# A retention and gated-MLP kernel: own output buffers and earlier transposes for the last batches, norms of first halves moved, last output unit in halves, another order in the head

## The chip, the cores and the metric

The kernel runs on one core of a Trainium2 chip. The metric is the device time of one execution in microseconds (us). Three runs of the kernel before gave 229.06, 230.06 and 230.72 us; their median, 230.06 us, is the time that the change is measured against. A difference of about 1% is what a measurement can tell from no change.

The engines are named as in the profile: PE (matrix multiply) with its weight loads PEld, DVE (vector), ACT (scalar), POOL (GpSimd) and SP, which here only issues transfers. Every engine works through its own list of instructions in order; semaphores connect the lists.

## The reference

Eight batches of eight heads, 576 positions, head width 64. Retention is attention without a softmax: the scores are weighted with a causal decay that has its own rate for each head. A gated MLP follows, whose gate mixes positions with a 576 x 576 matrix.

```python
scores = scale * np.matmul(q, k.transpose(0, 1, 3, 2))          # (8, 8, 576, 576)
Dmat = np.where(rel >= 0, gamma[:, None, None] ** rel, 0.0)      # rel = i - j
x = np.matmul(scores * Dmat, v)                                  # -> (8, 576, 512)
h = gelu_tanh(x @ w_in)                                          # (8, 576, 1024)
u, v = h[..., :512], h[..., 512:]
v_n = (v - mean(v)) / np.sqrt(var(v) + 1e-6) * g_ln
v_s = np.einsum('ts,bsd->btd', w_sg, v_n) + b_sg[None, :, None]
out = x + (u * v_s) @ w_out
```

## The kernel before

**Tiling.** The decay is split into one factor on q and one on k, so that retention becomes a running state. The 8 x 576 positions are worked off in 18 blocks. A group of four batches has one lead block (the first 64 positions of all four) and then two blocks of 256 positions for each batch, a first half and a second half. A block holds two chunks of 128 positions, c = 0 and 1. Two batches form a pair p with nine chunks; chunk 4 (`MID`) holds the leads of both. Blocks 10 to 17 are batches 4 to 7; the last two belong to batch 7.

**Steps of a block j.** `load` fetches q, k and v into the pool `ld` (three buffers of each tag; q and k share one tile of tag "qk", v has tag "vf"). `cast` scales them to bf16, on POOL from block 3 on. `T` (PE) or `turn` (a transposing transfer on SP's queue) transposes q and k. `Sc` makes the scores on PE and masks them on DVE (`ret`, L320). `Z` adds to the state and copies it to bf16 (`zb`, L344). `inter` and `intra` give the retention output in PSUM; two copies on ACT bring it to `xT` (L377). These copies go through the helper `copy`, so that the profile shows them under L245. `V` (L381) makes the second half of h: four matmuls `hv`, the gelu on ACT (`vg`), then `stats` on DVE (`bst`, `mv`, `rs`, and `vc`, which is the centred value times g_ln), `power` on POOL (`rs` to the power -1/2, L392) and `norm` on ACT (`vn`, or `vnm` for the lead chunk). `U` makes the first half (`hu`, `uT`).

**Steps of a batch.** When its second block is through, `release` queues eight units `W` (L440: the mixing of positions, five matmuls each, then a DVE product `gT`) and its units `O` (L459: four matmuls with w_out, the residual x, and the output transfer). `run(n)` takes n units from that queue at fixed places of a block; `slots` holds these numbers. A `W` needs the `vn` of all five chunks of its batch.

**The residual in O.** Where no transposed x is there, four matmuls with the identity add x in PSUM (L469) and ACT copies to `ob`. For batches 5 to 7 `turn_x` (L292) has asked SP's queue for the transpose of `xT`, and DVE adds it (L473). `ob` has three buffers for all units (pool `w3`); an `ob` is free again when its output transfer has ended.

**What sets the order.** The program is written out by hand, step by step (from L504; the blocks 3 to 17 in the loop at L627). `later(n, f)` (L231) postpones f by n ticks; each `T`, `V`, `U`, `W` and `O` ends with a tick. In the loop `stats` comes 2 and `norm` 4 ticks after `V`. In the head (blocks 0 to 2) they are called by name from `stats_of`, `pow_of` and `norm_of`. PSUM buffers of tag "d" (three) are shared by `hv`, `hu`, `wp` and `op`.

**The head** also prepares constants: `split_b` splits the bias into three bf16 rows, `place_b(e)` writes them into `wL[e]` with three small transfers issued by POOL, `load_w` fetches w_sg, `build_wT` transposes it, and `w_in` is cast by ACT and POOL. `spin(n)` issues n matmuls of zeros whose result nobody reads.

Of the kernel before, what the change touches and what calls it, by code (L numbers as in the profile page):

```python
# [19 lines left out]
def kernel(  # L20
# [77 lines left out]

    srow_i = consts.tile([128, 3, 2], I32, name="srow_i")
    nc.gpsimd.iota(srow_i[:, 0], pattern=[[1, 2]], base=0, channel_multiplier=2)  # L100
    nc.gpsimd.iota(srow_i[:, 1:], pattern=[[256, 2], [1, 2]], base=LEAD, channel_multiplier=2)
# [64 lines left out]
    bp = consts.tile([SB * 2, 3, 64], BF, name="bp")  # L166

# [122 lines left out]
    xns = {}  # L290
# [34 lines left out]
    def Z(j, c):  # L325

        gr, b, half = place(j)
        if b is None or (half, c) == (1, 1):
            nb = GB * gr if b is None else b + 1
            if c == 0 or nb == GB * (gr + 1):  # L330
                return
            src, lo, n, first = blk[NPG * gr], 32 * (nb % GB), 32, True
            zcur[0] = psZ.tile([128, KK, D], F32, name="zp")
        else:
            src, lo, n, first = blk[j], 64 * c, 64, False
        z, rows = zcur[0], slice(lo, lo + n)
        for a in range(2):
            for kk in range(KK):
                for r in range(2):
                    h = 2 * kk + r  # L340
                    nc.tensor.matmul(z[64 * r:64 * r + 64, kk, :], src["kb"][rows, a, h, :], src["vb"][rows, a, h, :],  # L341
                                     start=(first and a == 0 and kk == 0), stop=True, skip_group_check=True)
# [36 lines left out]
    stats_of, pow_of, norm_of = {}, {}, {}  # L379

    def V(j, c, wait=(2, 4)):  # L381
# [12 lines left out]
        def stats():  # L394
# [6 lines left out]
            st["rs"] = rs  # L401
            if wait:
                power()
            vc = w2.tile([128, F2], F32, name="vc")
# [15 lines left out]
        if wait:  # L420
            later(wait[0], stats)
            later(wait[1], norm)
        else:
            stats_of[2 * j + c], pow_of[2 * j + c], norm_of[2 * j + c] = stats, power, norm
# [34 lines left out]
    def O(p, m):  # L459
        op = psD.tile([128, DM], F32, name="op", tag="d")  # L460
        r = slice(128 * m, 128 * m + 128)
        xn = xns.get((p, m))
        for c in range(KK):
            nc.tensor.matmul(op[:], gTs[p][:, c, r], w_out[:, c, :], start=(c == 0),  # L464
                             stop=(xn is not None and c == KK - 1), skip_group_check=True)
        ob = w3.tile([128, DM], F32, name="ob")
        if xn is None:
            for kk in range(KK):
                nc.tensor.matmul(op[:, 128 * kk:128 * kk + 128], xTs[p][:, m, kk], ident[:],  # L469
                                 start=False, stop=True, skip_group_check=True)  # L470
            nc.scalar.copy(ob[:], op[:])  # L471
        else:
            nc.vector.tensor_tensor(ob[:], op[:], xn, op=Alu.add)  # L473
        if m == MID:
            for e in range(2):
                nc.sync.dma_start(out[2 * p + e, :LEAD, :], ob[64 * e:64 * e + 64])
        else:
            s0 = LEAD + 128 * (m % (MID + 1))
            nc.sync.dma_start(out[2 * p + (m > MID), s0:s0 + 128, :], ob[:])
# [34 lines left out]
    split_b()  # L514
# [10 lines left out]
    nc.gpsimd.memset(wnat[:, :, 0:64], 0.0)  # L525
    place_b(0)
# [5 lines left out]
    T(1, "q")  # L532
    cast(1, "v", nc.gpsimd)
# [3 lines left out]
    cast(2, "k", nc.gpsimd)  # L537
    inter(1)
# [3 lines left out]
    cast(2, "q", nc.vector)  # L542
    T(2, "k")
# [6 lines left out]
    for n in range(2):  # L550
        (nc.gpsimd.tensor_copy if n else nc.scalar.copy)(w_in[:, :, 256 * n:256 * n + 256], w_stage[0][:, :, 256 * n:256 * n + 256])
# [3 lines left out]
    Z(2, 0)  # L555
    inter(2)
    fill_first()
    stats_of[0]()
    pow_of[0]()
    Sc(2, 1)  # L560
    Z(2, 1)
    cast(3, "k", nc.gpsimd)
# [5 lines left out]
    U(0, 1)  # L568
    intra(2)
    U(1, 0)  # L570
    norm_of[2]()
    stats_of[3]()
    cast(3, "q", nc.gpsimd)
    pow_of[3]()
    V(2, 0, None)
    V(2, 1, None)
    load(5)
    build_wT(wb[0])
    norm_of[3]()
    U(1, 1)  # L580
    build_wT(wb[1])
    stats_of[4]()
    cast(3, "v", nc.gpsimd)
    place_b(1)
    pow_of[4]()
    build_wT(wb[2])
    U(2, 0)
    build_wT(wb[3])
    stats_of[5]()
    pow_of[5]()  # L590
    norm_of[4]()
# [28 lines left out]
    later(14, stats_of[1])  # L620
    later(16, pow_of[1])
# [5 lines left out]
    for j in range(HEAD, NB):  # L627
        nx = j + 1 < NB
        slots = where[share.get(j, 6)]
# [15 lines left out]
        if not nx:  # L645
            V(j, 1)
        run(slots[1])
# [15 lines left out]
        for x in {NB - 4: (NB - 6, NB - 5), NB - 3: (NB - 4,), NB - 2: (NB - 3, NB - 2), NB - 1: (NB - 1,)}.get(j, ()):  # L663
            turn_x(x)
# [37 lines left out]
```

## Time and profile before

| what | value |
|---|---|
| median of three runs (lowest, highest) | 230.06 us (229.06, 230.72) |
| the profiled execution's own time | 228.41 us |
| its span in the profile | 226.6 us |
| busy PE / DVE / POOL / ACT | 205.2 / 165.7 / 129.4 / 125.3 us |
| moved by transfers | 47.34 MB, mean 209 GB/s |
| longest groups by busy time on PE | `wp` 41.7, `hu` 37.8, `hv` 35.1, `op` 34.8 us |

A row of the timeline gives the start (us from the span's start), the busy time, the engine, the line, the operation with its output and inputs, and the count; in square brackets stands how long the engine was idle before it, and what ended that. A row of the windows gives a stretch, its length, and each engine's busy time in it with the number of instructions; then the clock granted to PE (1.00 is full), the share of time that the transfer engines were busy, and GB/s. A row of the waits gives the total idle time in us, the number of waits and the longest. The profiled execution took 1.8 us more than its span, and 1.65 us less than the median of the three runs.

### The profile page before, as it was taken

What the parts mean: (1) busy time and instruction counts of PE and PEld (TensorE: products, weight loads), DVE (VectorE), ACT (ScalarE), POOL (GpSimd) and SP (SyncE); (2) the same over time, 40 slices, a digit from 0 to 9 for tenths busy, and PEclk for the clock granted to TensorE, in tenths of its full rate; (3) what the DMA queues carried; (4) which work ended last, traced back from release to release, by engine and by line L of the source; (5) the groups of instructions that cost most, each with busy time, mean ns of one, the idle gap of its engine ahead of it and who ended that gap; (6) DMA issues with size and microseconds to landing.
All of it is one profiled execution on the core that took longest, in us unless ns stands there. A gap on an engine that the chain in (4) does not pass through costs nothing.

```text
span 226.6 us, 8008 instructions
## 1 busy us (share of the span) xinstructions
PE 205.2 (91%) x3391; PEld 145.5 (64%) x3427; DVE 165.7 (73%) x356; ACT 125.3 (55%) x202; POOL 129.4 (57%) x130
## 2 busy tenths in 40 slices
PE   7796998789999799999999799999999999799990
PEld 2444575577677587677677676777767766566650
DVE  5456599778969797469857866769856987777852
ACT  5353467715576755856594848675565546265110
POOL 5298759799956595729483847648482811113000
PEclk9999699999999999999999999999999999999998
DMA  7999999999999699799959999999989934822334
GB/s 174 279 304 277 304 254 280 278 248 227 168 243 298 166 201 208 235 204 314 220 168 275 235 208 146 241 245 258 222 228 200 133 69 117 210 49 46 139 99 183
DMA packets 87492, 47.34 MB, mean 209 GB/s; under 512 B 25440, under 2 KB 81824, under 8 KB 87456
## 3 DMA queue, kind: packets, MB, share of 16 engines
q1 hardware_dynamic: 84896, 45.10, 87.4%
q0 software_dynamic: 1472, 1.20, 3.4%
q10 hardware_dynamic: 1088, 0.52, 1.0%
q8 instruction: 27, 0.44, 0.9%
q14 instruction: 9, 0.07, 0.1%
HBM read 32.79 MB, written 9.44 MB: 186 GB/s over the span
## 4 chain that ended last, share of the span: by engine, by line
PE 54%; DMA 17%; POOL 11%; DVE 6%; ACT 4%; issue 3%; ACTq 1%; DVEq 0%; SPq 0%; POOLq 0%
PE wp L454 14%; PE op L464 9%; PE hv L385 9%; PE hu L434 9%; DMA qk<-in_q_dram 6%; DMA qk<-in_k_dram 5%; DMA out_dram<-ob 4%; POOL rs L392 3%; PE sc L316 3%; POOL kb L263 2%; PE ot L368 2%; PE ot L357 2%; PE zp L341 2%; POOL qb L263 2%; PE tp L272 2%
## 5 line engine op out<-in xcount | busy, mean ns | idle before, releaser
L392 POOL TENSOR_TENSOR rs<-rs,mhalf 128x1 f32<-128x1 f32 x36 | 33.0, 918 | 68.8 <-DVE rs L400 68.7
L320 DVE TENSOR_TENSOR ret<-sc,mask 128x512 bf16<-128x512 f32 x72 | 46.1, 683 | 9.6 <-PE sc L316 9.6
L454 PE MATMUL wp<-wT,vn 128*128 128x288 bf16 x256 | 41.7, 286 | 2.9 <-DMA wL<-bp 1.3
L434 PE MATMUL hu<-xT,w_in 128*128 128x128 bf16 x576 | 37.8, 219 | 1.4 <-DVE ob L473 1.4
L385 PE MATMUL hv<-w_in,xT 128*128 128x512 bf16 x125 | 35.1, 380 | 3.9 <-ACT xT L245 2.9
L434 PEld LDWEIGHTS <-w_in 128*128 128x128 bf16 x576 | 34.1, 98 | 4.1 <-issue 1.5
L456 DVE TENSOR_TENSOR gT<-wp,uT 128x288 bf16<-128x288 f32 x64 | 28.1, 452 | 11.6 <-PE wp L454 10.2
L396 DVE BATCH_NORM_STATS2 bst<-vg 128x6 f32<-128x512 f32 x36 | 24.8, 689 | 15.9 <-ACT vg L388 15.7
L464 PE MATMUL op<-w_out,gT 128*128 128x512 bf16 x129 | 34.8, 380 | 1.1 <-issue 0.5
L417 ACT ACTIVATE vn<-vc,rs 128x512 bf16<-128x512 f32 x32 | 23.1, 722 | 19.5 <-POOL rs L392 18.3
L263 POOL TENSOR_TENSOR kb<-qk,gk 128x1024 bf16<-128x1024 f32 x16 | 30.9, 1930 | 2.5 <-DMA qk<-in_k_dram 2.4
L405 DVE SCALAR_TENSOR_TENSOR vc<-vg,mv,g_bc 128x512 f32<-128x512 f32 x36 | 31.5, 875 | 0.2 <-issue 0.2
L454 PEld LDWEIGHTS <-vn 128*128 128x128 bf16 x256 | 23.8, 98 | 11.2 <-ACT vn L417 3.6
L388 ACT ACTIVATE vg<-hv 128x512 f32<-128x512 f32 x36 | 21.3, 595 | 16.8 <-PE hv L385 16.6
L263 POOL TENSOR_TENSOR qb<-qk,gq 128x1024 bf16<-128x1024 f32 x15 | 29.0, 1931 | 0.0
L437 ACT ACTIVATE uT<-hu 128x512 bf16<-128x512 f32 x36 | 21.7, 602 | 12.3 <-PE hu L434 12.2
L471 ACT COPY ob<-op 128x512 f32<-128x512 f32 x24 | 14.0, 589 | 19.8 <-PE op L469 19.0
L245 ACT CAST xT<-ot 128x512 bf16<-128x512 f32 x33 | 22.0, 730 | 2.1 <-PE ot L368 2.1
L385 PEld LDWEIGHTS <-xT 128*128 128x128 bf16 x144 | 13.0, 98 | 15.7 <-ACT xT L245 5.1
L245 ACT COPY kT<-tp 128x1024 bf16<-128x1024 bf16 x15 | 15.1, 1007 | 8.8 <-PE tp L272 8.8
L464 PEld LDWEIGHTS <-gT 128*128 128x128 bf16 x144 | 12.5, 98 | 10.9
L454 PE MATMUL wp<-wL,vnm 128*128 128x288 bf16 x64 | 18.4, 287 | 0.0
(96 smaller groups left out, 264.8 us busy)
## 6 DMA issues: line engine op xcount, KB each, us to landing
qk<-in_k_dram SPq DMA_DIRECT2D x16, 512.0 KB, 6.2
qk<-in_q_dram SPq DMA_DIRECT2D x16, 512.0 KB, 7.8
vf<-in_v_dram SPq DMA_DIRECT2D x16, 512.0 KB, 7.1
out_dram<-ob SPq DMA_DIRECT2D x32, 256.0 KB, 3.3
wst<-in_moe_w_in_dram SPq DMA_DIRECT2D x2, 1024.0 KB, 7.8
vf<-in_v_dram SPq DMA_DIRECT2D x8, 128.0 KB, 4.5
out_dram<-ob SPq DMA_DIRECT2D x8, 128.0 KB, 2.4
qk<-in_k_dram SPq DMA_DIRECT2D x6, 128.0 KB, 3.4
```

What stands on the lines that cost most here:

```text
L245: (eng.copy if eng is nc.scalar else eng.tensor_copy)(o, i)
L263: eng.tensor_tensor(o, src, tab[:, kind].rearrange("p a h -> p h a").unsqueeze(3).to_broadcast([128, H, 2, D]), op=Alu.mult)
L320: nc.vector.tensor_tensor(s["ret"][:, r, 2 * g:2 * g + 2], sc[r][:], msk[:].unsqueeze(1).to_broadcast([128, 2, 2, 128]), op=Alu.mult)
L385: nc.tensor.matmul(hv[:], xTs[p][:, m, kk], w_in[:, kk, F2:], start=(kk == 0), stop=(kk == KK - 1))
L392: nc.gpsimd.tensor_tensor(st["rs"][:], st["rs"][:], mhalf[:], op=Alu.pow)
L396: nc.vector.bn_stats(bst[:], vg[:])
L405: nc.vector.scalar_tensor_tensor(vc[:], vg[:], mv[:, 0:1], g_bc[:], op0=Alu.subtract, op1=Alu.mult)
L417: nc.scalar.mul(vn[:], vc[:], rs[:])
L434: nc.tensor.matmul(hu[:, c, :], w_in[:, kk, 128 * c:128 * c + 128], xTs[p][:, m, kk], start=(kk == 0), stop=(kk == KK - 1), skip_group_che ...
L454: nc.tensor.matmul(ps[:], vns[p, m][e][:, 128 * c:128 * c + 128], w, start=(x == 0), stop=(x == SB - 1))
L456: nc.vector.tensor_tensor(gTs[p][:, c, col:col + HS], ps[:], uTs[p][:, c, col:col + HS], op=Alu.mult)
L464: nc.tensor.matmul(op[:], gTs[p][:, c, r], w_out[:, c, :], start=(c == 0), stop=(xn is not None and c == KK - 1), skip_group_check=True)
```

## The change

1. **Output buffers.** For batches 5 to 7 the units `O` of whole chunks no longer write to `ob` but to `obs`, one tile per batch with a row for each of its four chunks, taken from the tag "qk" of the pool `ld`.
2. **Transposes of x.** `turn_x` is called after `V(j, 0)` instead of at the end of a block, and for blocks 12 and 13 in block 13 instead of block 14. `turn_mid` is new: it transposes the lead chunk of the last pair, whose unit `O` then uses DVE's addition instead of four identity matmuls and ACT's copy.
3. **Norms.** `norm` of the second chunk (c = 1) of first-half and lead blocks comes 6 ticks after `V` instead of 4. The calculation of `vc` becomes a function of its own, `centre`; in the loop it still follows `power` directly.
4. **Last unit.** The last `O` works in two halves of 256 columns, each with its own PSUM tile, addition and transfer; the second transfer is issued by ACT.
5. **Copies of the state.** From block 13 on ACT makes the copy `zb` (nine copies) instead of DVE.
6. **Last block.** `slots` of block 17 is (3, 0, 1, 1) instead of (2, 1, 1, 1): three units `W` stand ahead of its `V`.
7. **Head.** POOL: a doubled pair of index instructions goes; `split_b` moves from before the cast of w_in to between the casts of block 1's k and v, and its two clearings of `wL` are done in `clear_wL` too; `place_b(0)` moves to just ahead of the first `power`; the cast of block 3's k moves behind the first three `power`. DVE: the statistics of chunks 3, 4 and 5 (blocks 1 and 2) are taken earlier, ahead of a `vc` or of copies of w_sg that stood before them. ACT: its half of the first w_in cast moves behind two gelus and a `zb`. PE: two spins before `inter(1)` and four before `T(2, "k")`. `vc` of the lead chunk of pair 1 (`cen_of[1]`) is postponed to one tick after its statistics.

```diff
+    def clear_wL():
+        nc.gpsimd.memset(wL[0][64:], 0.0)
+        nc.gpsimd.memset(wL[1][:64], 0.0)
+        nc.gpsimd.memset(wnat[:, :, 0:64], 0.0)
...
+    def turn_mid(p):
+        xns[p, MID] = xn = consts.tile([128, DM], BF, name="xmid")
+        nc.sync.dma_start_transpose(xn[:].rearrange("p (k t) -> p k t", k=KK),
+                                    xTs[p][:, MID].rearrange("p k t -> p (k t)"))
...
-        copy(nc.scalar if j < 3 else nc.vector, zb[:], z[:])
+        copy(nc.scalar if j < 3 or j > NB - 6 else nc.vector, zb[:], z[:])
...
             if wait:
                 power()
+                centre()
+
+        def centre():
+            mv = st["mv"]
             vc = w2.tile([128, F2], F32, name="vc")
...
-            later(wait[1], norm)
+            later(wait[1] + 2 * (c - place(j)[2] > 0), norm)
...
     def O(p, m):
-        op = psD.tile([128, DM], F32, name="op", tag="d")
...
+        b, s0 = 2 * p + (m > MID), LEAD + 128 * (m % (MID + 1))
+        if xn is None or m == MID:
+            ob = w3.tile([128, DM], F32, name="ob")
         else:
+            if b not in obs:
+                obs[b] = ld.tile([128, MID, DM], F32, name="obs", tag="qk")
+            ob = obs[b][:, m % (MID + 1)]
+
+        n = 2 if (b, m) == (B - 1, NT - 1) else 1
+        for h in range(n):
+            op = psD.tile([128, DM // n], F32, name="op", tag="d")
+            f = slice(DM // n * h, DM // n * (h + 1))
...
+                (nc.scalar if h else nc.sync).dma_start(out[b, s0:s0 + 128, f], ob[:, f])
...
-    split_b()
+    clear_wL()
...
-    nc.gpsimd.memset(wnat[:, :, 0:64], 0.0)
-    place_b(0)
...
     T(1, "q")
+    split_b()
     cast(1, "v", nc.gpsimd)
...
     cast(2, "k", nc.gpsimd)
+    spin(2)
     inter(1)
...
     cast(2, "q", nc.vector)
+    spin(4)
     T(2, "k")
...
     fill_first()
+    place_b(0)
     stats_of[0]()
+    cen_of[0]()
     pow_of[0]()
...
     later(14, stats_of[1])
+    later(15, cen_of[1])
     later(16, pow_of[1])
...
-        slots = where[share.get(j, 6)]
+        slots = where[share.get(j, 6)] if nx else (3, 0, 1, 1)
...
+        for x in {NB - 5: (NB - 6, NB - 5)}.get(j, (j,) if j > NB - 5 else ()):
+            turn_x(x)
+        if j == NB - 3:
+            turn_mid(B // 2 - 1)
         run(slots[1])
...
-        for x in {NB - 4: (NB - 6, NB - 5), NB - 3: (NB - 4,), NB - 2: (NB - 3, NB - 2), NB - 1: (NB - 1,)}.get(j, ()):
-            turn_x(x)
```

More of the change, by code (lines that the diff above doesn't have):

```diff
@@ L459, in O @@
     def O(p, m):
-        op = psD.tile([128, DM], F32, name="op", tag="d")
         r = slice(128 * m, 128 * m + 128)
         xn = xns.get((p, m))
[L463 to L471, printed above, removed]
-        else:
-            nc.vector.tensor_tensor(ob[:], op[:], xn, op=Alu.add)
@@ new lines, in O @@
+        n = 2 if (b, m) == (B - 1, NT - 1) else 1
+        for h in range(n):
+            op = psD.tile([128, DM // n], F32, name="op", tag="d")
+            f = slice(DM // n * h, DM // n * (h + 1))
+            for c in range(KK):
+                nc.tensor.matmul(op[:], gTs[p][:, c, r], w_out[:, c, f], start=(c == 0),
+                                 stop=(xn is not None and c == KK - 1), skip_group_check=True)
+            if xn is None:
+                for kk in range(KK):
+                    nc.tensor.matmul(op[:, 128 * kk:128 * kk + 128], xTs[p][:, m, kk], ident[:],
+                                     start=False, stop=True, skip_group_check=True)
+                nc.scalar.copy(ob[:, f], op[:])
+            else:
+                nc.vector.tensor_tensor(ob[:, f], op[:], xn[:, f], op=Alu.add)
+            if m == MID:
+                for e in range(2):
+                    nc.sync.dma_start(out[2 * p + e, :LEAD, :], ob[64 * e:64 * e + 64])
+            else:
+                (nc.scalar if h else nc.sync).dma_start(out[b, s0:s0 + 128, f], ob[:, f])
@@ L549 @@
     cast(2, "v", nc.gpsimd)
-    for n in range(2):
-        (nc.gpsimd.tensor_copy if n else nc.scalar.copy)(w_in[:, :, 256 * n:256 * n + 256], w_stage[0][:, :, 256 * n:256 * n + 256])
+    nc.gpsimd.tensor_copy(w_in[:, :, :256], w_stage[0][:, :, :256])
     V(1, 0, None)
@@ L555 @@
     Z(2, 0)
+    nc.scalar.copy(w_in[:, :, 256:F2], w_stage[0][:, :, 256:])
     inter(2)
     fill_first()
+    place_b(0)
     stats_of[0]()
+    cen_of[0]()
     pow_of[0]()
@@ L561 @@
     Z(2, 1)
-    cast(3, "k", nc.gpsimd)
     wb = ["L0", "L1"] + list(range(SB - 1))
@@ L568 @@
     U(0, 1)
+    stats_of[3]()
     intra(2)
+    cen_of[2]()
+    pow_of[3]()
+    cast(3, "k", nc.gpsimd)
     U(1, 0)
     norm_of[2]()
-    stats_of[3]()
-    cast(3, "q", nc.gpsimd)
-    pow_of[3]()
+    cen_of[3]()
     V(2, 0, None)
     V(2, 1, None)
+    cast(3, "q", nc.gpsimd)
     load(5)
```

31 lines of the change are left out of this document (13 added, 18 removed).

## The prediction

> **What bounds the kernel now.** I read the span and PE's busy time by stage first, then what PE waited for, then the timeline around each of its waits.
>
> ```profile
> span 226.6 us, 8008 instructions
> ```
>
> ```profile
> 0.00:46.00 46.00, 37.84 (x553) 23.63 (x559) 31.88 (x68) 25.27 (x43) 32.92 (x53) 0.96 1.07 268
> 46.00:76.00 30.00, 26.99 (x559) 20.32 (x561) 25.25 (x51) 16.32 (x26) 25.47 (x23) 1.00 1.06 233
> 76.00:120.00 44.00, 43.53 (x735) 32.03 (x743) 31.98 (x71) 29.77 (x48) 27.50 (x21) 1.00 0.98 216
> 120.00:132.00 12.00, 10.41 (x199) 8.09 (x199) 8.39 (x20) 7.90 (x12) 6.62 (x5) 1.00 1.26 236
> 132.00:185.00 53.00, 52.26 (x988) 39.35 (x996) 40.67 (x92) 32.42 (x54) 31.32 (x24) 1.00 1.02 206
> 185.00:204.00 19.00, 17.07 (x256) 11.36 (x253) 14.66 (x31) 9.27 (x15) 3.69 (x4) 1.00 0.44 113
> 204.00:221.30 17.30, 17.15 (x126) 10.77 (x126) 11.57 (x24) 4.30 (x7) 1.85 (x2) 1.00 0.33 100
> 221.30:226.60 5.30, 0.00 (x0) 0.00 (x0) 1.29 (x2) 0.00 (x0) 0.00 (x0) 0.80 0.46 172
> ```
>
> From 76 us on PE sets the pace: it idles 0.5 us of 44, 0.7 of 53, 0.15 of 17.3. What it idles stands in few places: 8.2 us before 46, 3.0 up to 76, 1.6 around 130, 1.9 between 185 and 204, and the 5.3 after its last matmul. A wait taken away in a stage where PE is the pace moves everything behind it. So the question is which of PE's waits the change removes.
>
> ```profile
> PE hv L385 <- ACT xT L245: 2.9, 4, 1.5
> PE hu L434 <- DVE ob L473: 1.4, 1, 1.4
> PE wp L454 <- DMA wL<-bp: 1.3, 1, 1.3
> PE tp L272 <- DVE qb L263: 1.3, 2, 0.9
> PE wp L454 <- ACT vn L417: 1.2, 1, 1.2
> ```
>
> **Norms of first halves.** ACT works in order:
>
> ```profile
> 128.16 1.45 ACT L413 ACTIVATE vnm<-vc,rs 64x512 bf16<-64x512 f32 x2 [0.90 <-POOL rs L392]
> 129.64 1.32 ACT L245 CAST xT<-ot 128x512 bf16<-128x512 f32 x2
> ```
>
> Here the norm of block 9's second chunk waits 0.90 us for POOL, then takes 1.45, and only then come the copies `xT`, for which PE's `hv` waits 1.5 us. Nobody needs that `vnm` for some blocks yet. Two ticks later it stands behind the copies in ACT's list, so `xT` begins some 2 us sooner and the wait goes. The same pair, a first half's `vn` ahead of `xT`, makes the smaller waits of this group: 2.9 us in four waits, of which 0.8 at 35.47 is the head's own (quoted below) and stays. So 2.1 us can go. In block 17 a third `W` (five matmuls) now stands ahead of `V` and fills what is left. Late next: after an earlier `hv` the gelu meets the moved norm on ACT, which can hold it up for as much as the norm lasts, 1.45. I take 1.9; bounds 0.8 (half of the longest wait, nothing of the others) and 2.1.
>
> **Statistics of the lead chunk.** At 75.32 `W` waits 1.2 us for a `vn`.
>
> ```profile
> 71.05 1.31 DVE L405 SCALAR_TENSOR_TENSOR vc<-vg,mv,g_bc 128x512 f32<-128x512 f32 x1
> 72.29 0.68 DVE L396 BATCH_NORM_STATS2 bst<-vg 128x6 f32<-128x512 f32 x1
> ```
>
> That `vn` comes from the statistics at 72.29, which stand behind the `vc` of pair 1's lead chunk. With `cen_of[1]` a tick later they start at 71.05 and all behind them is 1.24 us earlier: I take 1.1, bounds 0 and 1.24. The postponed `vc` stands ahead of the next two `ret`, where it stood before as a sum, so these are no later.
>
> **Output buffers.**
>
> ```profile
> 194.89 0.69 DVE L473 TENSOR_TENSOR ob<-op,xn 128x512 f32<-128x512 f32 x1 [1.48 <-DMA out_dram<-ob]
> ```
>
> DVE waits 1.48 us until a transfer gives an `ob` back; PE's `hu` needs the PSUM tile that this addition frees, and waits 1.4. Each row of `obs` is written once and waits for no output transfer. The tile itself is the buffer of the q and k of blocks 15 to 17, cast blocks before. DVE also loses the `zb` that stands there between. I take 1.35, bounds 0 and 1.4.
>
> **The end.**
>
> ```profile
> 217.41 0.39 PE L469 MATMUL op<-ident,xT 128*128 128x128 bf16 x4
> 217.64 3.62 PE L464 MATMUL op<-w_out,gT 128*128 128x512 bf16 x16
> ...
> 219.57 0.69 DVE L473 TENSOR_TENSOR ob<-op,xn 128x512 f32<-128x512 f32 x1 [0.17 <-PE op L464]
> 221.71 1.29 DVE L473 TENSOR_TENSOR ob<-op,xn 128x512 f32<-128x512 f32 x2 [1.45 <-DMA out_dram<-ob]
> ```
>
> PE ends at 221.26, the last addition at 223.0, or 1.74 later, because two additions waited for buffers. After the change additions keep up with PE (0.69 against 0.9 for four matmuls), and behind the last matmul stand about 0.2 and a half addition of 0.35 (half of 0.69), with up to 0.2 of the other half: 0.55 to 0.75. That is about 1.1 less. The four identity matmuls go as well, some 0.25 to 0.39. I take 1.5 together. The last two transfers are half as large and leave from two queues, which I cost at nothing; bounds 0.4 (the buffer wait stays, the matmuls go) and 2.4.
>
> **The head** is moved most and gains least that I can see.
>
> ```profile
> 35.47 1.90 PE L385 MATMUL hv<-w_in,xT 128*128 128x512 bf16 x7 [0.81 <-ACT xT L245]
> ...
> 44.98 0.30 PE L454 MATMUL wp<-wT,vn 128*128 128x288 bf16 x1 [1.31 <-DMA wL<-bp]
> ```
>
> ```profile
> 33.22 2.41 DVE L405 SCALAR_TENSOR_TENSOR vc<-vg,mv,g_bc 128x512 f32<-128x512 f32 x1
> ...
> 40.70 0.74 DVE L405 SCALAR_TENSOR_TENSOR vc<-vg,mv,g_bc 128x512 f32<-128x512 f32 x1
> 41.47 0.56 DVE L245 COPY wT<-wtp 128x576 bf16<-128x576 bf16 x2
> 41.95 0.68 DVE L396 BATCH_NORM_STATS2 bst<-vg 128x6 f32<-128x512 f32 x1
> ```
>
> ```profile
> 39.84 1.63 POOL L191 DMA_DIRECT2D wL<-bp  x3
> 41.48 0.58 POOL L392 TENSOR_TENSOR rs<-rs,mhalf 128x1 f32<-128x1 f32 x1
> 43.26 0.92 POOL L392 TENSOR_TENSOR rs<-rs,mhalf 128x1 f32<-128x1 f32 x1 [1.20 <-DVE rs L400]
> ```
>
> The wait at 44.98 is put down to a transfer to `wL`, but this `W` reads `wL[0]`, filled long before; what ends there is the last `vn`: `rs` until 44.18, then ACT's `vn`. Its statistics (41.95) now come ahead of the copies `wT` (0.56), so `rs` and `vn` come about 0.55 sooner; the last `wT` copy then is the next to be late, since DVE's sum is the same. Gain 0.5. On the other side `place_b(0)` (1.63 of POOL, by its twin) now stands ahead of the first `rs`, which by way of `vnm`, `uT` and `xT` sets the wait at 35.47. POOL idled in this place before:
>
> ```profile
> POOL kb L263 <- DMA qk<-in_k_dram: 2.4, 2, 1.6
> ```
>
> and the 1.6 us that it waited for block 3's k cover the three issues, as that cast now stands behind. If this cover is gone, 1.63 are lost. `split_b` likewise fills POOL's wait for block 1's v. The transfers of `place_b(0)` land in time:
>
> ```profile
> wL<-bp POOLq DMA_DIRECT2D x6, 1.1 KB, 5.8
> xn<-xT SPq DMA_TRANSPOSE x6, 3.7
> ```
>
> they are issued ahead of the wait at 35.47 and first read at 45, and 5.8 us fit in between. The added spins run where PE waits; what they do to its clock:
>
> ```profile
> 23.00:26.50 3.50, 3.28 (x49) 2.22 (x48) 1.81 (x3) 1.57 (x2) 3.50 (x6) 0.51 1.04 339
> ```
>
> For 3.5 us PE had half its clock; with all of it the 3.28 us of work would be some 1.6 shorter. I still take nothing, because PE then only waits longer at 35.47, behind POOL's `rs`. Head together: 0.5 gained; bounds 1.3 gained (the whole wait at 44.98) and 1.7 lost.
>
> The Trainium skill, "TensorE: Matmul & The Clock Gate", Part 1, says that PE falls to half rate after an idle window of about 3.4 us and returns after a busy one; the half-rate stretch of 3.5 us agrees. By it the spins may keep the clock up, which is the low rival below.
>
> **Costed at nothing.** The transposes of blocks 12 and 13 now stand in SP's queue ahead of block 17's load of v, the transposes of 14 to 17 and the new one near where they were; an `xn` takes 3.7 us to land and is read blocks later. Its cover is the distance between a load and its cast; if that is gone, each transpose costs up to 3.7. The nine `zb` on ACT lie beside PE (ACT was busy 32.4 of 53 us); what they cost otherwise is a rival.
>
> **Sum.** 1.9 + 1.1 + 1.35 + 1.5 + 0.5 = 6.35 us. On the profiled execution (228.41, span 226.6) that gives 222.1; that execution lies 1.65 below the median of 230.06, for which I forecast 230.06 - 6.35 = **223.7**. By the good bounds it is 2.1 + 1.24 + 1.4 + 2.4 + 1.3 = 8.4, or 221.6; by the bad ones 0.8 + 0 + 0 + 0.4 - 1.7 = -0.5, or 230.6.
>
> **Rivals.**
>
> *The head runs at full clock and passes it on* (8%). For: the half-clock row. Against: the gate through `rs`. If that gate is not one, at most the 1.6 come on top, but no more than the 0.8 that PE waits at 35.47 would be spared beyond my 0.5: 223.7 - 0.8 = 222.9.
>
> *DVE and POOL get into each other's way in the head* (15%). A `vc` took 2.41 us beside a POOL cast and 0.74 without. Two `vc` now follow each other directly just where POOL casts block 3's k and q. One such stretch more costs 1.67 and takes the 0.5 with it: 223.7 + 2.2 = 225.9. Against: there were slow ones before, too. "Advanced Engine Details and Errata" of the Trainium skill, GPSIMD Details, says that POOL shares a read and a write interface with DVE and conflicts with DVE instructions of two SBUF inputs, which a `vc` is.
>
> *The transfers set the pace* (12%). Their busy share is 0.98 to 1.26 up to 185 us. If loads, not PE, pace that stretch, the gains before 185 (0.5, 1.1, and 1.5 of the 1.9) become waits for loads, and only 3.25 are left: 226.8; with one transpose of 3.7 in the way of a load, 230.5. Against: from 46 us on POOL, which takes the loads in, waits for none of k (2.4 us in two waits in all by the row above, both in the head, at 20.8 and 33.2).
>
> *ACT becomes the bound of the last blocks, and the kernel slower* (7%). The row of `zb` on ACT:
>
> ```profile
> L245 ACT CAST zb<-zp 128x256 bf16<-128x256 f32 x5 | 1.9, 372 | 5.4 <-PE zp L341 5.4
> ```
>
> In order on ACT a `zb` waits until PE has done `Z`: 5.4 us in four waits, 1.35 each, and 0.37 of its own, with `vg`, `uT` and `vn` behind it. Up to 1.72 for each of nine. From four on the path all gains are eaten; with six it is 223.7 + 10.3 = 234.0. Against: in the loop `Z` follows `Sc` directly on PE, while ACT is still at two `xT` of 1.32.
>
> *The change doesn't do what it says* is part of the bounds: an `obs` that still waits leaves 1.35 + 1.1 unearned, 226.2; I count it with the forecast's upper side.
>
> **How the numbers follow.** Forecast with its near surroundings 58%, rivals 8, 15, 12 and 7%. Faster by over 1% (below 227.8, 1% being about what a measurement tells from no change): 58 + 8 + 15 and a third of 12, 0.85. Within 1%: the rest of that rival, 0.08. Slower by over 1% (above 232.4): 0.07. The range goes from 221.0, just under the good bounds, to 227.8, leaving out the last two cases for the most part.
>
> **What would show it.** Right: no wait of `hv` for `xT` above 0.5 us around 130; no wait of DVE for an output transfer; no wait of `W` for `vn` near 75; the last addition within 0.8 us of PE's end; PE's end near 216 (221.26 less the gains ahead of it). Wrong: PE waiting for `vg` or `vn` in blocks 13 to 17, POOL waiting for loads after 46, `vc` above 2 us three or more times in the head, or a first `W` later than 45.5.

## The result and the profile after

The changed kernel took 221.82 us (median of four runs, 219.89 to 226.09) beside 229.88 us for the kernel before, 8.1 us less; the ratio is 0.9621, 95% interval 0.9544 to 0.9698. The ratio leaves out the run of 226.09 us, which was in a slower state. A later measurement in five rounds gave 0.9711 (0.9684 to 0.9738), or 6.6 us less; its interval is narrower, and the variants below are set against that one. The forecast was 6.35 us less and 223.7 us. The profiled execution took 222.15 us against 228.41 us; its span is 6.2 us shorter.

First the page's head line of the changed kernel, then its windows up to PE's end, with the columns and, up to 204 us, the stretches of the prediction.

```profile
span 220.4 us, 8017 instructions
```

```profile
0.00:46.00 46.00, 38.38 (x564) 23.90 (x571) 31.49 (x69) 26.13 (x43) 33.20 (x53) 1.00 1.04 267
46.00:76.00 30.00, 28.76 (x577) 21.68 (x581) 26.45 (x54) 17.89 (x29) 27.10 (x23) 1.00 1.05 242
76.00:120.00 44.00, 43.58 (x773) 32.51 (x782) 32.34 (x73) 28.51 (x46) 26.57 (x20) 1.00 0.98 225
120.00:132.00 12.00, 11.63 (x224) 9.09 (x220) 10.59 (x24) 8.11 (x13) 9.37 (x7) 1.00 1.16 267
132.00:185.00 53.00, 51.78 (x942) 38.59 (x950) 36.73 (x80) 35.55 (x63) 29.13 (x24) 1.00 1.01 201
185.00:204.00 19.00, 18.84 (x266) 13.02 (x269) 15.86 (x36) 10.43 (x18) 4.43 (x5) 1.00 0.36 95
204.00:215.70 11.70, 11.49 (x73) 6.96 (x72) 9.26 (x18) 0.72 (x1) 0.18 (x1) 1.00 0.38 124
```

PE's idle time went where the prediction looked for it: 3.0 to 1.2 us between 46 and 76, 1.6 to 0.4 around 126, 1.9 to 0.2 between 185 and 204. It grew from 0.7 to 1.2 between 132 and 185, which was not foreseen. What PE waited for, over the whole execution and then from 46 us on:

```profile
PE hv L391 <- ACT xT L246: 1.5, 3, 0.8
PE zp L347 <- POOL vb L246: 0.8, 1, 0.8
```

```profile
PE wp L466 <- ACT ob L493: 0.5, 1, 0.5
```

The 1.5 us of `hv` are the head's. The waits of `hu` for an addition and of `W` for `wL` are gone. The wait of `zp` for block 1's v is 0.8 us instead of 0.3, and the 0.5 for ACT's `ob` is new.

To see where the 6.2 us arose, a second reading counts the gelus `vg` on ACT, 36 in all and in the same order in every kernel, and subtracts their starts. The last row but one is the end of the last addition on DVE. The spans are given to a tenth, so the last step is rounded.

| vg number (what) | before, us | after, us | earlier by | step |
|---|---|---|---|---|
| 1 (block 0) | 16.36 | 17.13 | -0.77 | first loads later here |
| 7 (block 3) | 56.00 | 55.39 | 0.61 | +1.38, head |
| 9 (block 4) | 66.07 | 64.74 | 1.33 | +0.72 |
| 11 (block 5) | 77.80 | 75.23 | 2.57 | +1.24, lead statistics |
| 20 (block 9) | 125.26 | 122.54 | 2.72 | +0.15 |
| 28 (block 13) | 166.38 | 162.41 | 3.97 | +1.25, norms |
| 32 (block 15) | 187.64 | 184.03 | 3.61 | -0.36 |
| 34 (block 16) | 199.16 | 194.07 | 5.09 | +1.48, buffers |
| last addition | 223.00 | 216.14 | 6.86 | +1.77, end |
| span | 226.6 | 220.4 | 6.2 | about -0.6, last transfer |

**Norms.** ACT now makes `xT` first and the `vnm` behind it, and neither waits:

```profile
124.47 1.33 ACT L246 CAST xT<-ot 128x512 bf16<-128x512 f32 x2
125.83 1.45 ACT L423 ACTIVATE vnm<-vc,rs 64x512 bf16<-64x512 f32 x2
```

**Lead statistics.** The two groups on DVE have changed places; two `vc` follow them:

```profile
69.72 0.68 DVE L402 BATCH_NORM_STATS2 bst<-vg 128x6 f32<-128x512 f32 x1
...
70.80 1.40 DVE L415 SCALAR_TENSOR_TENSOR vc<-vg,mv,g_bc 128x512 f32<-128x512 f32 x2
```

**Buffers and end.** No addition waits for a transfer, and PE's last group runs without a gap:

```profile
188.79 1.28 DVE L495 TENSOR_TENSOR obs<-op,xn 128x512 f32<-128x512 f32 x2
...
211.13 4.49 PE L487 MATMUL op<-w_out,gT 128*128 128x512 bf16 x23
...
214.79 1.35 DVE L495 TENSOR_TENSOR obs<-op,xn 128x512 f32<-128x512 f32 x3 [0.17 <-PE op L487]
```

The last addition ends at 216.14, 0.5 us behind PE. The span ends 4.2 us after that, against 3.6 us before.

**The head.** The last `vn` for the first `W` now makes a wait of 0.27 us instead of 1.31:

```profile
44.38 0.30 PE L466 MATMUL wp<-wT,vn 128*128 128x288 bf16 x1 [0.27 <-ACT vn L427]
```

### The profile page after: what moved, and what is told of

It reads as the page before. It is cut to its first block, busy times and chain, and to the rows that moved or that the text cites. A ratio compares the mean times of both kernels' runs of the same rounds, so it can differ in the third digit from the quotient of the medians.

```text
span 220.4 us, 8017 instructions
## 1 busy us (share of the span) xinstructions
PE 204.5 (93%) x3396; PEld 145.7 (66%) x3433; DVE 163.2 (74%) x349; ACT 127.3 (58%) x210; POOL 130.0 (59%) x130
## 4 chain that ended last, share of the span: by engine, by line
PE 68%; DVE 11%; DMA 8%; POOL 5%; ACT 3%; issue 2%; ACTq 0%; DVEq 0%; POOLq 0%; SPq 0%
PE wp L466 17%; PE op L487 12%; PE hu L446 11%; PE hv L391 10%; DMA wst<-in_moe_w_in_dram 3%; PE ot L374 3%; PE sc L322 3%; PE zp L347 3%; PE ot L363 3%; PE tp L273 3%; DVE vc L415 2%; DVE bst L402 2%; DMA qk<-in_q_dram 2%; DVE ret L326 2%; DMA out_dram<-ob 2%
## 5 line engine op out<-in xcount | busy, mean ns | idle before, releaser
L398 POOL TENSOR_TENSOR rs<-rs,mhalf 128x1 f32<-128x1 f32 x36 | 31.9, 886 | 64.0 <-DVE rs L406 58.1
L487 PE MATMUL op<-w_out,gT 128*128 128x512 bf16 (+1 forms) x133 | 34.7, 374 | 1.1 <-issue 0.5
L264 POOL TENSOR_TENSOR kb<-qk,gk 128x1024 bf16<-128x1024 f32 x16 | 31.4, 1963 | 0.7 <-ACT xT L246 0.7
L493 ACT COPY ob<-op 128x512 f32<-128x512 f32 x23 | 13.5, 587 | 11.6 <-PE op L491 9.7
```

The source lines that it names most:

```text
L264: eng.tensor_tensor(o, src, tab[:, kind].rearrange("p a h -> p h a").unsqueeze(3).to_broadcast([128, H, 2, D]), op=Alu.mult)
L398: nc.gpsimd.tensor_tensor(st["rs"][:], st["rs"][:], mhalf[:], op=Alu.pow)
L487: nc.tensor.matmul(op[:], gTs[p][:, c, r], w_out[:, c, f], start=(c == 0), stop=(xn is not None and c == KK - 1), skip_group_check=True)
```

## The experiments

Six kernels take one part of the change back, three alter it further, one adds a single part to the kernel before, and two are the changed kernel again. Ratios are to the kernel before, run beside them; 0.001 is 0.23 us.

| kernel | median, us | ratio (95% interval) | vg 7 behind vg 1, us | last addition to span's end, us |
|---|---|---|---|---|
| before, profiled | 229.88 | 1 | 39.64 | 3.6 |
| after, profiled | 221.82 | 0.9621 (0.9544 to 0.9698) | 38.26 | 4.2 |
| changed, second time | 220.91 | 0.9726 (0.9659 to 0.9793) | 37.22 | 4.2 |
| changed, third time | 221.65 | 0.9711 (0.9684 to 0.9738) | 37.34 | 4.3 |
| norms back | 223.93 | 0.9813 (0.9766 to 0.9861) | 37.20 | 4.3 |
| lead statistics back | 222.27 | 0.9735 (0.9684 to 0.9785) | 37.19 | 4.3 |
| buffers back | 222.58 | 0.9744 (0.9694 to 0.9793) | 37.28 | 3.1 |
| head back | 223.34 | 0.9780 (0.9738 to 0.9821) | 39.72 | 4.5 |
| spins out | 221.68 | 0.9726 (0.9679 to 0.9773) | 39.61 | 4.3 |
| `zb` back on DVE | 220.99 | 0.9719 (0.9666 to 0.9772) | 37.73 | 4.4 |
| last lead `O` earlier | 222.34 | 0.9716 (0.9635 to 0.9797) | 39.93 | 3.5 |
| no second clears | 220.79 | 0.9675 (0.9627 to 0.9723) | 40.61 | 4.4 |
| four alterations | 219.93 | 0.9646 (0.9611 to 0.9682) | 37.71 | 3.5 |
| before with spins | 227.88 | 1.0003 (0.9973 to 1.0033) | 39.32 | 3.7 |

The last two columns are of one profiled execution each. Executions differ in when the first loads land: the first `vg` came between 16.2 and 18.3 us. So profiles are compared from a `vg` on, not from zero.

### The changed kernel again

> The changed kernel once more, unaltered, to have its time and its tail on the same chip as the variants beside it. Theory (the ratio of 0.962 holds): 0.962 of the kernel before. The last addition ends 4.3 us before the span does, as in the other runs with buffers of their own, against 3.1 us where the ring of three was put back.

The theory's 0.962 was not met: the ratio came out higher, 0.9726, with 0.962 outside its interval. The tail is the same, 4.2 us.

> The changed kernel unaltered a third time, in five rounds, for a narrower ratio: the first gave 0.962, the second 0.973. Theory (executions differ by when the first loads land and by where the clock falls, which puts single times 1 to 3 us apart): the ratio lies between the two, 0.965 to 0.972, and above that of the version with four things altered, 0.9646. Rival (the first ratio is the kernel's): 0.960 to 0.964, and the version with four things altered is no better.

0.9711: within the range that the theory gave. The change is worth about 2.9%; the interval of the first ratio, up to 0.9698, reaches just into this one.

### Norms of first halves back

```diff
-            later(wait[1] + 2 * (c - place(j)[2] > 0), norm)
+            later(wait[1], norm)
```

> The changed kernel, but the norms of first halves come at their old tick (the third W of block 17 stays ahead of V). Theory (a norm ahead of the xT copies on ACT is what PE waited for): PE waits again 1.5 us for xT in the block whose second chunk is a lead one (near 126 us), and some 0.4 us in smaller waits; 221.8 + 1.9 = 223.7. Rival (the waits went because statistics and copies come earlier for other reasons, or the norm moved from one wait to another): no wait of hv for xT above 0.5 us after the head, 221.8 to 222.2.

The waits are back, and there are two of that size. Of ACT, then of PE, in this variant:

```profile
62.87 0.72 ACT L427 ACTIVATE vn<-vc,rs 128x512 bf16<-128x512 f32 x1 [1.25 <-POOL rs L398]
...
126.19 1.45 ACT L423 ACTIVATE vnm<-vc,rs 64x512 bf16<-64x512 f32 x2 [0.90 <-POOL rs L398]
```

```profile
64.27 1.04 PE L391 MATMUL hv<-w_in,xT 128*128 128x512 bf16 x4 [1.71 <-ACT xT L246]
...
128.45 1.04 PE L391 MATMUL hv<-w_in,xT 128*128 128x512 bf16 x3 [1.48 <-ACT xT L246]
```

The one at 128.45 is the wait of the prediction, row for row. The one at 64.27 is the same pair in block 4; in the kernel before it cost only 0.23, since POOL's `rs` came in time there. The ratio says 0.9813 less 0.9711, or 2.3 us, against 1.9 forecast; in the profiles the last addition comes 2.5 us later than in the second measurement and 3.3 later than in the third, counted from `vg` 1. The mechanism is shown.

### Statistics of the lead chunk back

```diff
-    later(15, cen_of[1])
+    later(14, cen_of[1])
```

> The changed kernel, but the vc of pair 1's lead chunk again directly behind its statistics, one tick earlier than in the changed kernel. Theory: the next statistics start about 1.2 us later and W waits 1.2 us for a vn near 73 us; PE is 1.1 to 1.24 us later from there to the end, 222.9. Rival (what ended that wait is POOL or ACT, which the new head order made earlier): no wait over 0.5 us for a vn between 70 and 77 us, 221.8.

DVE, then PE, in this variant:

```profile
68.08 1.31 DVE L415 SCALAR_TENSOR_TENSOR vc<-vg,mv,g_bc 128x512 f32<-128x512 f32 x1
69.31 0.68 DVE L402 BATCH_NORM_STATS2 bst<-vg 128x6 f32<-128x512 f32 x1
```

```profile
72.35 0.30 PE L466 MATMUL wp<-wT,vn 128*128 128x288 bf16 x1 [0.80 <-ACT vn L427]
```

The wait returns, with 0.80 us at PE. From `vg` 9 to `vg` 11 this variant loses 1.22 us on the changed kernel of the second measurement. At the last addition 0.4 of that is left, counted from `vg` 1. But against the third measurement, the same kernel, 1.2 is left. The two references differ between `vg` 28 and 32, where the second measurement waits 1.14 us for an `ob` and the third does not wait (shown below, with the state copies). The ratios differ by 0.0024 (0.5 us) and their intervals overlap. So the place is shown; how much of its gain reaches the end is not.

### Output buffers back

```diff
-        if xn is None or m == MID:
+        if True:
```

> The changed kernel, but every output tile again comes from the ring of three buffers; the rest, last unit in halves included, stays. Theory (the buffers of their own give 1.35 us at the waiting addition and 1.1 us at the end): DVE waits again about 1.5 us for an output transfer ahead of the gelu work near 190 us, PE's hu waits 1.4 us behind it, the last additions wait again over 1 us; 221.8 + 1.35 + 1.1 = 224.3. Rival (the nine zb copies that left DVE, or transfers that start sooner, took the waits away, and the buffers are not needed): no such wait over 0.5 us, 221.8.

DVE and PE of this variant:

```profile
189.05 0.69 DVE L495 TENSOR_TENSOR ob<-op,xn 128x512 f32<-128x512 f32 x1 [1.41 <-DMA out_dram<-ob]
...
215.34 0.69 DVE L495 TENSOR_TENSOR ob<-op,xn 128x512 f32<-128x512 f32 x1 [1.47 <-DMA out_dram<-ob]
216.57 0.76 DVE L495 TENSOR_TENSOR ob<-op,xn 128x256 f32<-128x256 f32 x2 [0.54 <-DMA out_dram<-ob]
```

```profile
189.80 1.05 PE L446 MATMUL hu<-xT,w_in 128*128 128x128 bf16 x16 [0.91 <-DVE ob L495]
```

All three waits are back: 1.07 us at `vg` 34 and 3.0 us in all at the last addition (217.33 less 214.88, plus the 0.56 that this execution was ahead of the second measurement at `vg` 33). But its span ends only 3.07 us after the addition, not 4.2, so 1.1 of the 3.0 is given back in the last transfer, and 1.9 is left where the theory had 2.45. The ratios differ by 0.0033, or 0.8 us, with overlapping intervals. What takes the rest is in the transfer view; median us from issue to landing of the last transfer, in the changed kernel, with the buffers back, and in the next variant:

```profile
out_dram<-obs ACTq DMA_DIRECT2D x1, 128.0 KB, 2.9
```

```profile
out_dram<-ob ACTq DMA_DIRECT2D x1, 128.0 KB, 1.8
```

```profile
out_dram<-obs ACTq DMA_DIRECT2D x1, 128.0 KB, 2.1
```

The rate from 212 to 227 us, in 40 equal slices, of the changed kernel and then with the buffers back:

```profile
GB/s 0 0 0 0 0 131 191 197 197 377 393 371 382 393 339 344 183 19 0 0 0 0 0 0 0 0 0 0 0 0 0 0 0 0 0 0 0 0 0 0
```

```profile
GB/s 0 0 0 131 191 208 202 361 388 377 230 22 11 360 333 120 322 262 0 0 0 0 0 0 0 0 0 0 0 0 0 0 0 0 0 0 0 0 0 0
```

Where the ring of three holds the additions up, there are gaps between transfers (22 and 11 GB/s); without it, nearly 1 MB leaves in one train of seven slices at 339 to 393 GB/s, and the last transfer stands behind the others. The Trainium skill, "DMA: Bandwidth & Descriptors", in its opening table, gives some 358 GB/s as the limit of HBM for one core; five slices of the train lie above that, at 371 to 393, so here, with one core running, it is no sharp limit.

### The last lead unit earlier

```diff
+            if b == B - 1 and len(ws) == 4:
+                wo.append(own.pop(0))
```

> The changed kernel with the O of the last lead chunk ahead of the last four W instead of behind them. Nothing else moves. Theory (the last transfer is slow because 1.28 MB of output leave in under 5 us): one transfer of 256 KB leaves about 2.5 us sooner, PE's end stays, the last transfer takes 2.2 us instead of 2.9, and the span ends 0.5 to 0.8 us sooner. Rival (the last transfer's time is its own, from ACT's queue, whatever goes on beside it): the span ends as before, 4.3 us behind the last addition.

The last transfer took 2.1 us instead of 2.9, and the span ended 3.5 us behind the last addition instead of 4.2: 0.7 us, as the theory said. This execution's head was 2.7 us slower (below), and the ratio, 0.9716, shows nothing either way; the gain at the end rests on this profile and on that of the four alterations, which include this one and end 3.5 us behind as well.

### The state copies back on DVE

```diff
-        copy(nc.scalar if j < 3 or j > NB - 6 else nc.vector, zb[:], z[:])
+        copy(nc.scalar if j < 3 else nc.vector, zb[:], z[:])
```

> The changed kernel with the nine zb copies of the last blocks on DVE again instead of ACT. Theory (they lie beside PE on either engine): every vg from block 13 on within 0.3 us of the changed kernel's, time the same within 0.5 us. Rival (on ACT they hold up gelu and norms): without them the last blocks are 0.5 us or more faster. Rival (DVE needs the room): PE waits for additions or ret, 0.5 us or more slower.

Ratio 0.9719 beside 0.9726 in the same group of runs. From `vg` 28 to `vg` 32 this variant gains 0.52 us on the changed kernel of the second measurement, which is what the first rival said. But it waits 0.60 for an `ob` where that one waits 1.14, and the changed kernel of the third measurement, with its copies on ACT, does not wait and gains 0.96 in the same stretch. The rows of this variant, of the second and of the third measurement:

```profile
167.18 0.59 ACT L493 COPY ob<-op 128x512 f32<-128x512 f32 x1 [0.60 <-DMA out_dram<-ob]
```

```profile
167.49 0.59 ACT L493 COPY ob<-op 128x512 f32<-128x512 f32 x1 [1.14 <-DMA out_dram<-ob]
```

```profile
166.35 0.61 ACT L493 COPY ob<-op 128x512 f32<-128x512 f32 x1
```

So the copies themselves cost nothing that shows on either engine. The wait is the loss of 0.36 us in the table of steps: batch 4's outputs still use the ring of three. It comes and goes. Of the eleven profiles of the changed kernel and its variants with three buffers, ACT waits there in eight and PE behind it in three; in the kernel before, with or without spins, neither does. That PE, nearly 4 us earlier, now meets these transfers is likely, but not shown.

### The head: order and clock

Head back:

```diff
-    clear_wL()
+    split_b()
...
-    place_b(0)
     stats_of[0]()
...
-    stats_of[3]()
     intra(2)
-    cen_of[2]()
...
     build_wT(wb[3])
+    stats_of[5]()
+    cen_of[5]()
+    pow_of[5]()
```

with all other steps of the head, the spins among them, in the order of before.

> The changed kernel with the order of the head as before (spins, split_b, place_b(0), statistics, copies and casts up to the last transposed weight block), the loop and the end as changed. Theory (the head gives 0.5 us, by statistics that come ahead of the wT copies; the clock gives nothing): the first gelu of block 3 is 0.5 to 0.7 us later, 222.3, though PE's clock falls to half for some microseconds before 27 us. Rival (the clock is what the head gains by): a half-clock stretch of 3.5 us returns and everything from 35 us on is 1.3 to 1.6 us later, 223.3. Rival (contention of DVE and POOL in the new order costs what the rest gains): no later or even earlier, 221.8 or less.

Spins out:

```diff
     cast(2, "k", nc.gpsimd)
-    spin(2)
...
-    spin(4)
     T(2, "k")
```

> The changed kernel without the six added spin matmuls of the head. Theory (a lower clock there only shortens a wait that PE has anyway at 36 us): the profile may show a stretch at half clock before 27 us, the first gelu of block 3 (line 394, the seventh vg) comes within 0.3 us of where it is with the spins, counted from the first vg, and the time is the same within 0.5 us. Rival (the clock is what the new head gains by): that gelu comes 1.0 to 1.6 us later, and so does the end.

Before with spins:

```diff
     cast(2, "k", nc.gpsimd)
+    spin(2)
...
+    spin(4)
     T(2, "k")
```

> The kernel before with the six added spin matmuls of the head and nothing else of the change. Theory of the prediction (PE's clock only lengthens a wait that is set elsewhere): the clock row from 23 to 26.5 us is near 1.00, the vg of V(2,0) comes 20.3 us behind the first vg as before, within 0.4 us, and the time is that of the kernel before within 0.5 us. Theory formed since (the chain that ends in the wait at 35 us begins with PE's own work before 27 us, so that a slow clock there is passed on whole): that vg comes 18.5 to 19.0 us behind the first, and the time is 1.3 to 1.9 us below the kernel before.

The windows of the changed kernel (first profile), of spins out, and of before with spins (PE's clock is the third column from the right):

```profile
23.00:26.50 3.50, 3.34 (x94) 2.35 (x90) 2.42 (x3) 1.40 (x3) 3.50 (x7) 1.00 1.08 378
```

```profile
20.00:23.00 3.00, 2.28 (x64) 2.11 (x64) 1.01 (x2) 0.50 (x2) 2.23 (x3) 0.64 1.06 281
23.00:26.50 3.50, 3.31 (x45) 2.02 (x45) 1.87 (x3) 1.25 (x2) 3.50 (x6) 0.50 1.08 357
26.50:30.00 3.50, 3.50 (x47) 1.81 (x49) 2.52 (x4) 1.46 (x3) 2.79 (x6) 0.83 1.18 236
```

```profile
23.00:26.50 3.50, 3.40 (x68) 2.07 (x61) 2.95 (x4) 2.01 (x3) 3.50 (x6) 1.00 1.10 381
42.00:45.00 3.00, 1.36 (x15) 0.73 (x12) 2.02 (x6) 2.40 (x5) 1.81 (x2) 1.00 1.15 279
45.00:48.50 3.50, 3.50 (x25) 2.90 (x26) 1.28 (x3) 1.01 (x1) 3.50 (x3) 0.51 1.13 288
```

Read these with the column "vg 7 behind vg 1". Order alone (spins out): 39.61 us, as before's 39.64. Spins alone: 39.32. Both together: 37.2 to 37.7 in seven profiles; 38.3 in the first one, where block 1's q took 9.8 us to land instead of 8.4; 39.9 and 40.6 in two where loads were late and the clock fell. Head back: 39.72, some 2.4 us behind the second and third measurement. Of these 2.4, 1.2 are the first `W`, whose wait returns:

```profile
45.14 0.30 PE L466 MATMUL wp<-wT,vn 128*128 128x288 bf16 x1 [1.50 <-ACT vn L427]
```

**What the clock does.** In the new order, without the spins, PE is at half clock from about 21 to 28 us. The `vg` of block 2's first V then comes 21.07 us behind the first `vg`, instead of 18.90 in the second measurement; counted from the start of the span it is 1.8 us later. The prediction let the wait at this V take up such a gain. It does not: the wait is 0.80 us with the spins (first row) and without them (second row), as it was 0.81 in the kernel before.

```profile
34.41 1.90 PE L391 MATMUL hv<-w_in,xT 128*128 128x512 bf16 x8 [0.80 <-ACT xT L246]
```

```profile
36.22 1.90 PE L391 MATMUL hv<-w_in,xT 128*128 128x512 bf16 x8 [0.80 <-ACT xT L246]
```

The rows of ACT in the kernel before say why:

```profile
32.24 0.60 ACT L437 ACTIVATE uT<-hu 128x512 bf16<-128x512 f32 x1 [0.57 <-PE hu L434]
32.73 1.44 ACT L413 ACTIVATE vnm<-vc,rs 64x512 bf16<-64x512 f32 x2
34.20 0.60 ACT L437 ACTIVATE uT<-hu 128x512 bf16<-128x512 f32 x1
34.69 0.72 ACT L245 CAST xT<-ot 128x512 bf16<-128x512 f32 x1
```

The last wait of ACT ahead of this `xT` is for PE's own `hu`; `vnm` does not wait for POOL's `rs`. So the wait moves along with PE, and a slow clock ahead of it is passed on, 1.8 to 2.2 us here.

In the old order the spins also keep the clock up at 23 us, but that pair shows little: the same `vg` comes 18.2 us behind the first instead of 20.3, the first `vg` was 1.9 us later, and counted from the start of the span only 0.2 us are gained (36.47 against 36.70). Then PE still waits for the first `W`, is busy for 1.36 us of 3, and falls to half clock right after, at 45 us. In this profile the half-clock stretch has only moved.

The times say less. Spins alone: 1.0003, no gain, so the theory formed since, with 1.3 to 1.9 us, failed on the time. Spins out: 0.9726, the same as the changed kernel beside it. Head back: 0.9780 against 0.9711, 1.6 us, with intervals that just touch; its 223.34 us is what the rival of the clock said, but it takes back the order and the spins together. So the head as a whole is worth 1.4 us in the first pair of profiles, about 2.4 in the later ones and 1.6 by the ratios. The mean granted clocks of the executions fit a gain through the clock in the new order only: 0.991 to 1.000 in the second measurement beside 0.981 to 0.997 with spins out; but 0.982 to 0.999 before with spins beside 0.984 to 1.000 before, with a median of 0.991 in both. That the spins decide it in every execution is not shown: the clock held in some runs without them (a mean of 0.997 in one run of spins out) and fell in one with them (0.66 from 23 to 26.5 in the profile of the last lead `O` earlier, where block 1's loads were late).

### Two further alterations and all four together

```diff
     def split_b():
-        nc.gpsimd.memset(wL[0][64:], 0.0)
-        nc.gpsimd.memset(wL[1][:64], 0.0)
```

> The changed kernel without the two clears of wL in split_b, which clear_wL has done before. Theory (these clears keep POOL from the cast of block 1's v, for which Z waits 0.7 to 1.0 us): the wait of zp for vb goes, later work up to 45 us comes 0.5 to 0.8 us sooner, counted from the first vg, and the end too. Rival (what comes next is late anyway, block 2's q from its load): nothing before the end is more than 0.2 us sooner.

The wait of `zp` for block 1's v did not go. POOL and PE of this variant:

```profile
19.09 1.04 POOL L244 CAST vb<-vf 128x1024 bf16<-128x1024 f32 x1 [0.54 <-DMA vf<-in_v_dram]
```

```profile
20.18 0.44 PE L345 MATMUL zp<-vb,kb 64*64 64x64 bf16 x16 [1.11 <-POOL vb L244]
```

POOL is ready 0.54 us before that load lands, so a load sets the place. In kind the rival holds there, though it named block 2's q. In this execution the second w_in load was late as well, and PE lost its clock at 36 us, hence 40.61. The ratio, 0.9675, lies under the changed kernel's 0.9711 with overlapping intervals.

```diff
-            ob = w3.tile([128, DM], F32, name="ob")
+            ob = w3.tile([128, DM], F32, name="ob", bufs=4)
...
     T(1, "k")
+    spin(1)
     T(1, "q")
...
     Sc(1, 0)
+    spin(1)
     Z(1, 0)
```

and the two edits shown above.

> The changed kernel with four things: no second clears of wL in split_b; four instead of three buffers of ob (left takes one of them in the head); the O of the last lead chunk ahead of the last four W; one spin each ahead of T(1,q) and Z(1,0). Theory: 0.5 us in the head, 0.5 to 1.0 us near 169 us, where ACT waits for an output transfer to give an ob back and PE for ACT, 0.6 us at the end: 1.6 to 2.1 us below the changed kernel, 0.7% to 0.9%. Rival (a fourth ob only moves the wait to the transfers behind it): 1.1 us.

0.9646 (0.9611 to 0.9682), just clear of the changed kernel's 0.9684 to 0.9738: 1.5 us faster than it, between the theory's 1.6 and the rival's 1.1. With four buffers the copy near 167 us waits for nothing:

```profile
166.58 0.62 ACT L491 COPY ob<-op 128x512 f32<-128x512 f32 x1
```

Between `vg` 28 and 32 it gains 0.96 us on the changed kernel of the second measurement. But the third measurement, with three buffers, gains the same 0.96 there, so the profiles do not show what the fourth buffer is worth: it takes away a wait that some executions have and others have not. What they show is 0.7 us between the last addition and the end. The head gained nothing (37.71).

## Why the prediction came out right, point by point

- **The bound.** PE's waits, stage by stage, were the right place to look: five steps of the table are the five terms, and their signs hold. The signs named for a right prediction came as well, the last addition 0.5 us behind PE's end among them.
- **Norms, forecast 1.9.** Mechanism shown by taking it back: 1.5 us in the pair (1.25 at block 9, and 0.23 of the 0.72 at block 4, of which another 0.41 was a wait for `ret` behind a slow `vc`, which comes back with the head), so 0.4 less than forecast. Taking it back costs more, 2.3 us by the ratios, because in the changed kernel a late `rs` makes block 4's wait 1.71 instead of 0.23.
- **Lead statistics, forecast 1.1.** 1.24 in the pair, and 1.22 where it was taken back, both at the place itself. By the ratios 0.5, with overlapping intervals.
- **Buffers, forecast 1.35.** 1.48 in the pair, 1.07 where they were taken back.
- **The end, forecast 1.5.** 1.77 at the last addition (forecast as 1.1 and 0.25 to 0.39), but the step that cost the last transfers at nothing failed: they took about 0.6 us more, since the buffers that free DVE also bunch the outputs. Net about 1.2. The identity matmuls, the halves of the last unit, the earlier transposes and the third `W` of the last block were not taken back one by one.
- **The head, forecast 0.5.** 1.4 in the pair, 1.6 by the ratios; the bound of 1.3 was passed. The step that failed is "the last `wT` copy then is the next to be late": nothing came late there, and the whole wait but 0.27 went. The second step that failed is the reason for costing the spins at nothing, "PE then only waits longer at 35.47, behind POOL's `rs`": that wait stays at 0.80 us, since ACT waits there for PE's `hu`, and it moves along with PE by 1.8 to 2.2 us between the changed kernel with and without the spins. In the old order the spins gain no time all the same (1.0003); in the one profile of it the clock falls later.
- **Not foreseen:** the wait for an `ob` near 168 us, -0.36 in the pair. The prediction took the ring of three to be free wherever it was free before. In the changed kernel it is free in some executions and not in others.
- **Rivals.** The state copies on ACT do not bind. Transfers do not set the pace: after 46 us no cast of POOL waits for a load. The contention of DVE and POOL is there, below, but the first `W` came earlier all the same. The head at full clock did occur, and in the later profiles the head gains 2.4 us, more than the 0.8 us beyond the 0.5 that was allowed for it; whether this reaches the time in full is not shown.
- **The sum**, 6.35, stands against 8.1 us by the first medians, 6.6 by the third ratio and 6.2 in the pair, or 7.0 there without the later start. That it lies so close is partly luck, for errors of both signs cancel: in the pair the head was 0.9 too low, the norms 0.4 and the end 0.3 too high, and the `ob` 0.36 unseen. By the ratios, the four parts that cost time when they were taken back add up to 5.2 us (2.3, 0.5, 0.8 and 1.6).

## What to carry to other kernels

Price a removed wait at its place, then walk on to the next gate that the earlier program will meet, the output transfers above all: gains here were partly given back twice, at a buffer ring further on (in some executions) and in the last transfer. Ask of a wait whether it stays or moves when the waiting engine comes earlier: follow the engine it waits for back to that engine's own last wait. Idle matmuls that keep the clock up in one stretch need not gain time: alone they gained none here (1.0003). A wait that differs between two executions of the same kernel proves nothing about a variant. And where executions start at different times, compare profiles from a common instruction on, counting one kind of instruction through the program.

## What the runs showed of the hardware

**The clock can fall after a part-idle stretch, not only after a wholly idle one.** In the kernel before with spins PE was busy for 1.36 us of the 3 from 42 to 45, with no single wait over 1.51 us, and ran at 0.51 for the next 3.5. The Trainium skill, "TensorE: Matmul & The Clock Gate", Part 1, puts the fall after an idle window of about 3.4 us; the length of the slow stretch agrees, the idle window was not wholly idle here. The kernel before, with 1.37 us busy of the same 3, kept its clock, so the share alone does not decide, and what does is not shown:

```profile
42.00:45.00 3.00, 1.37 (x16) 0.73 (x13) 2.09 (x7) 2.58 (x5) 1.80 (x3) 1.00 1.07 274
45.00:48.50 3.50, 3.50 (x64) 2.93 (x65) 2.47 (x5) 1.01 (x1) 3.50 (x3) 1.00 0.84 231
```

**A `vc` on DVE is slow beside a cast on POOL.** The changed kernel's DVE and POOL, where two `vc` stand beside the cast of block 3's k, and that cast in the kernel before, beside the `vc` of 2.41 us at 33.22:

```profile
35.39 3.08 DVE L415 SCALAR_TENSOR_TENSOR vc<-vg,mv,g_bc 128x512 f32<-128x512 f32 x2
```

```profile
35.45 2.47 POOL L264 TENSOR_TENSOR kb<-qk,gk 128x1024 bf16<-128x1024 f32 x1
```

```profile
33.15 1.93 POOL L263 TENSOR_TENSOR kb<-qk,gk 128x1024 bf16<-128x1024 f32 x1 [1.62 <-DMA qk<-in_k_dram]
```

The pair of `vc` takes 3.08 us instead of 1.40 (the pair at 70.80 above), so DVE pays some 1.7 us in either kernel. The cast took 2.47 us in the changed kernel but 1.93 in the kernel before, which is also the mean of these casts on its page: that POOL pays as well is seen only in the first of the two, and why is not shown.
